# One piece of a down product moved behind the second group spot, sums of x one piece earlier, and the last unit's add of two copies moved up

## The chip, the cores and the metric

The kernel runs on one core of a Trainium2 chip, as a single launch. Its time is the device time of that core in microseconds (us). The engines of the core are named as the profile names them: TensorE (PE, with PEld for its weight loads), VectorE (DVE), ScalarE (ACT), GpSimd (POOL) and SyncE (SP). GpSimd issues the loads, SyncE issues the stores and the transposes done by DMA.

## The reference

Two layers follow each other. The first is attention with projected keys and values, over 8 batches, 8 heads, a sequence of 1024 and a head size of 64; keys and values are projected from 1024 rows to 64. The second is a maxout layer on the 8192 x 512 matrix that the attention gives.

```python
k_proj = einsum('ks,bhsd->bhkd', E, k)          # 64 x 64 for each head
v_proj = einsum('ks,bhsd->bhkd', F, v)
scores = matmul(q, k_proj.T) / sqrt(64)
attn   = exp(scores - max) / sum(exp(scores - max))
x      = matmul(attn, v_proj)                   # laid out as 8192 x 512
out    = maximum(x @ w1, x @ w2) @ w_out        # 512 -> 1024 -> 512, float32
```

The inputs are float32; the kernel computes in float16 with float32 accumulation.

## The kernel before

**The algebra.** `maximum(h1, h2)` is `relu(h1 - h2) + h2`. So the kernel works with `wd = w1 - w2` for the way up, and with `m = w2 @ w_out` for the part of the way down that needs no maximum: `out = relu(x @ wd) @ w_out + x @ m`. The way up and the way down are each done as a product of 2 x 2 blocks with seven products in place of eight (the Winograd form of Strassen's scheme). The names `p1` to `p7` in the code are these seven products; `s_x`, `s_g`, `t_w` and `T_sb` are the sums and differences of blocks of x, of the relu's output g, and of the weights that the scheme needs. The sums of x (`sums_x`) and of g (`sums_g`) are made by VectorE (line 519).

**Units.** A batch has two units, so there are sixteen, with the numbers 0 to 15; unit 1 is the second of batch 0 and unit 2 the first of batch 1. Each unit has an up phase (`up_steps`, matmuls at line 558) and a down phase (`down_steps`, matmuls at line 636). The down phase of unit n runs interleaved with the up phase of unit n + 1 and with attention for later units. Every down product is twelve matmuls, cut into three pieces of four (two pieces in unit 0, one in the last unit); so a unit has 21 down pieces, which are keyed `("P", n, product, piece)`, both counted from 0. The up phase has two halves of seven products each, keyed `("U", n, half, k)`. The order of the seven in both phases is 1, 2, 6, 5, 7, 3, 4.

**Group spots.** In each unit there are two places, `("G", n, 0)` and `("G", n, 1)`, at which attention work for one group of four heads stands: the scores of a new group (line 266) into the PSUM banks 2 and 3, and the sums and values of the group before it (line 278) into a pair of banks called `att`. ScalarE takes the exponential of the two score banks (line 355), then the logarithm of the sums (line 374); VectorE later multiplies the values by the inverse (line 381). At the second spot of unit 1 the sums and values stand ahead of the scores, and the scores there are the first of tile 2, whose `qt` comes from two DMA transposes that SyncE issues at the first spot of unit 1 (line 249).

**Banks.** The up products use banks 2 and 3, the same that the scores use; the first up product of the first half begins in bank 2, that of the second half in bank 3. The down products use banks 0 and 1. A product that is accumulated further must first be copied out of its bank: `keep` (line 529), on ScalarE. The first up product behind a group spot therefore waits until the exponential has emptied its bank, and the third up product of a half waits until the copy of the first is done.

**Order.** The order on every engine is written out by hand: a list `slots` is built once, each entry a piece, an up product or a spot, and `at_slot` hangs further work behind an entry (the sums, the projections of the next batch's k and v at line 180, their transposes at line 211, the loads). Engines keep this order and wait by semaphore. The list for unit n is made in the loop at lines 782 to 799: `x` pieces, the group spot, `y` pieces, then seven up products with one piece between each two. Unit 1 has its own pair of `(x, y)`.

**The last unit.** It has no up phase beside it. Product 7 (`p7`) is copied out as `u2`, product 5 as `s5`; product 3 (`p3`) is added to `u1` for the output block (0, 1), and then `u2 + s5` gives block (1, 1), both at line 660; product 4 is done in two halves, each added to `u2` (line 699). Every block is stored from SyncE as soon as it is added (line 651), blocks of 256 KB and the two halves of 128 KB.

Of the kernel before, what the change touches and what calls it, by code (L numbers as in the profile page):

```python
# [16 lines left out]
def kernel(  # L17
# [42 lines left out]
    def mm_bank(dtype=FP32, n=None):  # L60
        if n is None:
            n = turn.pop(0)
            turn.append(n)
        return ps.tile([128, 512 if dtype == FP32 else 1024], dtype, tag=f"mm{n}", name="mm_ps")
# [391 lines left out]
    U = {(b, o): {"n": n, "b": b, "o": o, "t": tiles[b]} for n, (b, o) in enumerate(units)}  # L456
# [28 lines left out]
    def s_g(i):  # L485
        return box[2].rearrange("q (s n m) -> q s n m", s=4, n=NG)[:, i]

    def s_x(i, u):
        n = u["n"] % 3
        half = box[1 if n < 2 else 3].rearrange("q (h s n m) -> q h s n m", h=2, s=4, n=NX)  # L490
        return half[:, n % 2, i]
# [10 lines left out]
    def x_blk(u, j, h):  # L502
        return u["t"]["xt"][:, h * NX : (h + 1) * NX, j, u["o"] * W : (u["o"] + 1) * W]

    def g_blk(u, j, h):
        if u["b"] == 0:
            return u["t"]["gt", u["o"]][:, h * NG : (h + 1) * NG, j * W : (j + 1) * W]
        return u["gt"][:, h * NG : (h + 1) * NG, j * W : (j + 1) * W]
# [18 lines left out]
    def keep(tag, bank, copy=nc.scalar.copy):  # L527
        x = ppool.tile([128, 512], FP32, tag=tag, bufs={"pu": 3, "pd": 4}[tag], name="p_sb")
        copy(out=x, in_=bank)  # L529
        return x  # L530
# [79 lines left out]
    def down_steps(u, alone):  # L610
        b, o = u["b"], u["o"]
        st = {}
        xbank, ybank = (0, 1) if u["n"] % 2 == 0 else (1, 0)

        def cat(g, x):
            return lambda n: g[:, n] if n < NG else x[:, n - NG]

        def product(k, name, n, lo=0, hi=2 * (NG + NX)):
            if n is not None and (lo == 0 or alone):
                st[name] = mm_bank(n=n)  # L620
            bank = st[name]
            A = lambda j, h: cat(g_blk(u, j, h), x_blk(u, j, h))
            S = lambda i: cat(s_g(i), s_x(i, u))
            Bb = lambda h, c: cat(
                wo_sb[:, h * NG : (h + 1) * NG, c * CH : (c + 1) * CH],
                m_sb[:, h * NX : (h + 1) * NX, c * CH : (c + 1) * CH],
            )
            T = lambda i: lambda n: T_sb[:, i, n, :]
            a, w_ = {
                1: lambda: (A(0, 0), Bb(0, 0)), 2: lambda: (A(0, 1), Bb(1, 0)),  # L630
                3: lambda: (S(3), Bb(1, 1)), 4: lambda: (A(1, 1), T(3)),
                5: lambda: (S(0), T(0)), 6: lambda: (S(1), T(1)), 7: lambda: (S(2), T(2)),
            }[k]()
            for m in range(lo, hi):
                i, c = divmod(m, NG + NX)
                nc.tensor.matmul(  # L636
                    out=bank[:, i * CH : (i + 1) * CH],
                    lhsT=a(c)[:, i * 128 : (i + 1) * 128],
                    rhs=w_(c),
                    start=(n is not None and m == (lo if alone else 0)),  # L640
                    stop=(c == NG + NX - 1), skip_group_check=True,
                )
            return bank

        two = lambda ap: ap.rearrange("q (i m) -> q i m", i=2)

        def o_tile():
            return opool.tile([128, 2, CH], FP32, tag="o", name="o_sb")

        def store(j, c, o_sb, i0=0, i1=2):  # L650
            nc.sync.dma_start(
                out=out.rearrange("(n p i o) m -> n o p i m", p=128, i=NI, o=2)[
                    b, j, :, 2 * o + i0 : 2 * o + i1, c * CH : (c + 1) * CH
                ],
                in_=o_sb[:, i0:i1],
            )

        def add(j, c, x, y):
            o_sb = o_tile()
            nc.vector.tensor_tensor(out=o_sb, in0=two(x), in1=two(y), op=ALU.add)  # L660
            store(j, c, o_sb)

        def keep_d(bank):
            return keep("pd", bank, *([nc.vector.tensor_copy] if u["n"] == 0 else []))

        size = 2 * (NG + NX) // (1 if alone else 2 if u["n"] == 0 else 3)

        def piece(k, name, n, m):
            product(k, name, n, m, m + size)

        def whole(k, name, n):
            return product(k, name, n, 2 * (NG + NX) - size)

        def p1():
            st["s1"] = keep_d(whole(1, "X", xbank))

        def p2():
            add(0, 0, whole(2, "Y", ybank), st["s1"])

        def p6():  # L680
            st["u1"] = keep_d(whole(6, "X", None))

        def p5():
            st["s5"] = keep_d(whole(5, "Z", ybank))

        def p7():
            st["u2"] = keep_d(whole(7, "X", None))

        def p3():
            add(0, 1, whole(3, "Z", None), st["u1"])  # L690
            add(1, 1, st["u2"], st["s5"])

        def p4():
            o_sb = o_tile()
            if alone:
                for i in range(2):
                    bank = product(4, ("C", i), 2 + i, 6 * i, 6 * i + 6)
                    part = slice(i * CH, (i + 1) * CH)
                    nc.vector.tensor_tensor(
                        out=o_sb[:, i], in0=bank[:, part], in1=st["u2"][:, part], op=ALU.add,  # L700
                    )
                    store(1, 0, o_sb, i, i + 1)
                return
            nc.scalar.copy(out=o_sb, in_=two(whole(4, "X", None)))
            store(1, 0, o_sb)

        steps_ = (
            (p1, 1, "X", xbank), (p2, 2, "Y", ybank), (p6, 6, "X", None), (p5, 5, "Z", ybank),
            (p7, 7, "X", None), (p3, 3, "Z", None), (p4, 4, "X", None),
        )  # L710
        return [
            (*(lambda a=a, m=m: piece(*a, m) for m in range(0, 2 * (NG + NX) - size, size)), f)
            for f, *a in steps_
        ]
# [67 lines left out]
    for n, key in enumerate(units):  # L782
        downs = down_steps(U[key], n == last)
        if n in (0, last):
            for p, pieces in enumerate(downs):
                slots += [(("P", n, p, i), x) for i, x in enumerate(pieces)]
            continue
        pieces = [(("P", n, p, i), x) for p, x in enumerate(downs) for i, x in enumerate(x)]
        ups = [*up_steps(U[units[n + 1]])]
        for h, (x, y) in enumerate(((3, 3), (2, 1)) if n == 1 else ((2, 2), (2, 3))):  # L790
            slots += pieces[:x]
            slots.append((("G", n, h), lambda: None))
            slots += pieces[x : x + y]
            del pieces[: x + y]
            for i in range(7):
                slots.append((("U", n, h, i), ups.pop(0)))
                if i < 6:
                    slots.append(pieces.pop(0))
        assert not pieces and not ups
# [3 lines left out]
    def at_slot(key, s, *a):  # L803
        steps.setdefault(key, []).append(lambda: s(*a))
# [47 lines left out]
    for b in range(3, B):  # L852
        t = tiles[b]
        n = 2 * b - 3
# [8 lines left out]
    for i, (new, old) in enumerate(zip([*groups[1:], none], groups)):  # L863
        n, h = divmod(i + 2, 2)
# [6 lines left out]
    for n, (b, o) in enumerate(units):  # L871
        u = U[b, o]

        if b == 0:
            where = ()
        elif n == 2:
            where = (("P", 1, 0, 2), 0), (("P", 1, 1, 0), 1), (("P", 1, 1, 2), 2), (("U", 1, 0, 1), 3)
        else:
            where = tuple((("U", n - 2, 1, k), i) for k, i in ((6, 2), (3, 0), (4, 1), (5, 3)))
        for key, i in where:  # L880
            at_slot(key, sums_x, u, (i,))

        if n:
            end = ("U", n - 1, 1, 6) if n > 1 else ("P", 0, 6, 1)
            m = 0 if n == last else 2
            for key, i in (end, 0), (("P", n, 0, 0), 1), (("P", n, 1, m), 2), (("P", n, 2, m), 3):
                at_slot(key, sums_g, u, (i,))
# [41 lines left out]
```

## Time and profile before

| | |
|---|---|
| median of 4 runs | 329.36 us (327.85 to 330.14) |
| the profiled execution's own time | 328.24 us |
| its span in the profile | 326.5 us |
| granted TensorE clock | 0.998 |
| TensorE busy | 317.0 us, 97% of the span |
| VectorE, ScalarE, GpSimd busy | 239.6, 201.1, 37.0 us |
| unit 1's down phase on TensorE | from about 64.5 to 84 us |
| last matmul begins; last engine work (VectorE) ends | 321.8; 322.8 us |

The span is what the hardware profiler shows of one execution; the execution's own time has some 1.7 us more around it. A line of the timeline gives start, duration, engine, line of the code, operation, what is written and read, and in brackets the idle time of that engine just before it and what ended that. A busy TensorE isn't the same as TensorE at its peak, since matmuls overlap and their ends are modelled; the steps from one start to the next are the better measure. PE and PEld are one engine's matmuls and its weight loads; `SPq` rows are DMA issues from SyncE.

### The profile page before, as it was taken

How to read it: one execution, taken by the hardware profiler on the slowest of the kernel's cores; microseconds unless marked ns; L12 is line 12 of the kernel's file. 1: busy time of each engine (PE TensorE's matmuls, PEld its weight loads, DVE VectorE, ACT ScalarE, POOL GpSimd, SP SyncE). 2: the span in 40 equal slices, each digit the busy share in tenths (PEclk: the TensorE clock that was granted, in tenths of full speed). 3: DMA queues.
4: the chain of work that ended last, by engine and by line, in shares of the span. 5: the costliest groups of instructions: out<-in, count | busy, mean ns of one | idle time of the engine just before them, and what ended most of it. 6: DMA issues, size and time to landing. Idle time of an engine off the chain costs nothing.

```text
span 326.5 us, 9015 instructions
## 1 busy us (share of the span) xinstructions
PE 317.0 (97%) x3856; PEld 248.6 (76%) x3856; DVE 239.6 (73%) x424; ACT 201.1 (62%) x359; POOL 37.0 (11%) x56
## 2 busy tenths in 40 slices
PE   7979999999999999999999999999999999999994
PEld 3544446877887788878887888878887888888883
DVE  1346898985969778677967796977967796969572
ACT  2365322666777577667776777657776777765541
POOL 8546002003000110003000300003000000000000
PEclk9999999999999999999999999999999999999999
DMA  8999999988999699997999599888999130312032
GB/s 147 204 197 191 206 207 208 218 197 150 194 238 233 115 158 238 202 187 97 215 217 180 110 187 243 190 163 125 228 192 214 37 99 32 98 34 98 33 131 96
DMA packets 74680, 53.14 MB, mean 163 GB/s; under 512 B 29456, under 2 KB 74512, under 8 KB 74640
## 3 DMA queue, kind: packets, MB, share of 16 engines
q0 software_dynamic: 29376, 28.31, 54.7%
q1 hardware_dynamic: 45264, 24.25, 30.7%
q8 instruction: 30, 0.49, 0.6%
q14 instruction: 10, 0.08, 0.1%
HBM read 57.15 MB, written 16.78 MB: 226 GB/s over the span
## 4 chain that ended last, share of the span: by engine, by line
PE 79%; DMA 13%; POOL 2%; DVE 2%; issue 1%; ACT 0%; DVEq 0%; POOLq 0%
PE mm_ps L636 44%; PE mm_ps L558 26%; DMA q_sb<-in_q_dram 8%; DMA v_sb<-in_v_dram 4%; PE att_ps L180 3%; PE att_ps L278 3%; PE mm_ps L266 3%; DMA big<-in_moe_w_dram 2%; POOL q_sb L102 1%; POOL k_sb L102 1%; DVE gt_sb L573 1%; PE mm_ps L237 1%; DVE o_sb L660 1%; POOL v_sb L102 1%; DVE xt_sb L381 0%
## 5 line engine op out<-in xcount | busy, mean ns | idle before, releaser
L529 ACT COPY p_sb<-mm_ps 128x512 f32<-128x512 f32 x172 | 97.1, 594 | 43.0 <-PE mm_ps L558 30.7
L636 PEld LDWEIGHTS <-big 128*128 128x128 f16 x768 | 73.5, 98 | 12.1 <-issue 3.5
L636 PE MATMUL mm_ps<-T_sb,big 128*128 128x256 f16 x576 | 77.9, 273 | 0.0
L573 DVE TENSOR_TENSOR gt_sb<-mm_ps,p_sb 128x512 f16<-128x512 f32 x56 | 38.5, 688 | 45.7 <-PE mm_ps L558 42.5
L558 PE MATMUL mm_ps<-big,big 128*128 128x256 f16 x336 | 50.4, 272 | 0.0
L558 PEld LDWEIGHTS <-big 128*128 128x128 f16 x448 | 43.8, 98 | 5.3 <-issue 0.2
L636 PEld LDWEIGHTS <-gt_sb 128*128 128x128 f16 x384 | 35.7, 98 | 9.6 <-issue 5.4
L636 PE MATMUL mm_ps<-wo_sb,gt_sb 128*128 128x256 f16 x256 | 42.9, 273 | 0.1
L558 PEld LDWEIGHTS <-wd_sb 128*128 128x128 f16 x336 | 32.9, 98 | 4.1 <-issue 0.4
L558 PE MATMUL mm_ps<-xt_sb,wd_sb 128*128 128x256 f16 x224 | 33.6, 273 | 0.2 <-ACT ex_sb L355 0.2
L355 ACT ACTIVATE ex_sb<-mm_ps 128x512 f16<-128x512 f32 x50 | 27.2, 597 | 9.6 <-PE att_ps L278 7.0
L381 DVE TENSOR_TENSOR xt_sb<-att_ps,ld_sb 128x1024 f16<-128x1024 f32 x26 | 31.7, 1219 | 0.1
L660 DVE TENSOR_TENSOR o_sb<-mm_ps,p_sb 128x512 f32<-128x512 f32 x32 | 21.9, 684 | 11.0 <-PE mm_ps L636 7.6
L636 PE MATMUL mm_ps<-m_sb,xt_sb 128*128 128x256 f16 x128 | 24.4, 273 | 0.0
L608 ACT ACTIVATE gt_sb<-mm_ps 128x512 f16<-128x512 f32 x28 | 16.8, 600 | 8.7 <-PE mm_ps L558 8.7
L519 DVE TENSOR_TENSOR big<-gt_sb 128x1024 f16<-128x1024 f16 x32 | 21.9, 685 | 0.2
L576 DVE TENSOR_SCALAR gt_sb<-gt_sb 128x512 f16<-128x512 f16 (+1 forms) x56 | 20.5, 366 | 1.9
L636 PE MATMUL mm_ps<-T_sb,gt_sb 128*128 128x256 f16 x128 | 21.5, 273 | 0.0
L636 PE MATMUL mm_ps<-wo_sb,big 128*128 128x256 f16 x128 | 21.5, 273 | 0.0
L636 PEld LDWEIGHTS <-xt_sb 128*128 128x128 f16 x192 | 18.8, 98 | 2.2
L229 POOL COPY junk<-kpt_sb 1x1 f16<-1x1 f16 x5 | 0.9, 176 | 162.0 <-DMA kpt_sb<-kp_sb 162.0
L573 DVE TENSOR_TENSOR gt_sb<-p_sb 128x512 f16<-128x512 f32 x28 | 19.1, 681 | 0.0
(85 smaller groups left out, 427.8 us busy)
## 6 DMA issues: line engine op xcount, KB each, us to landing
out_dram<-o_sb SPq DMA_DIRECT2D x63, 256.0 KB, 2.7
k_sb<-in_k_dram POOLq DMA_DIRECT2D x7, 1024.0 KB, 10.1
v_sb<-in_v_dram POOLq DMA_DIRECT2D x7, 1024.0 KB, 17.7
q_sb<-in_q_dram POOLq DMA_DIRECT2D x7, 1024.0 KB, 22.3
k_sb<-in_k_dram POOLq DMA_DIRECT2D x4, 256.0 KB, 6.8
q_sb<-in_q_dram POOLq DMA_DIRECT2D x4, 256.0 KB, 7.9
v_sb<-in_v_dram POOLq DMA_DIRECT2D x2, 512.0 KB, 12.5
big<-in_moe_w_dram POOLq DMA_DIRECT2D x8, 128.0 KB, 10.6
```

Of the source, the lines that this page charges most:

```text
L102: nc.gpsimd.dma_start(out=t[n][:, h0:h1], in_=src[b, h0:h1].rearrange("h (p c) d -> p h c d", c=NC),)
L180: nc.tensor.matmul(out=kv_ps[r * KP : (r + 1) * KP, 0:n], lhsT=eft[:, i, c, :], rhs=t[w][:, h0:h1, c, :], start=(c == 0), stop=(c == NC - 1),)
L355: nc.scalar.activation(out=t["ex", g, j][:, e, :], in_=banks[e], func=ACTF.Exp, scale=scale)
L381: nc.vector.tensor_tensor(out=x_out(t, g, j).rearrange("q z o n -> q o z n"), in0=at_ps.rearrange("q o (z n) -> q o z n", z=2), in1=ld[:, ...
L519: nc.vector.tensor_tensor(out=S(i), in0=x, in1=y, op=op)
L529: copy(out=x, in_=bank)
L558: nc.tensor.matmul(out=bank[:, m * W : (m + 1) * W], lhsT=w_[:, n_, (2 * d + m) * 128 : (2 * d + m + 1) * 128], rhs=a[:, n_, :], start=(n ...
L573: nc.vector.tensor_tensor(out=c_blk(j, c), in0=two(x), in1=two(y), op=ALU.add)
L576: nc.vector.tensor_scalar_max(ap, ap, 0.0)
L608: nc.scalar.activation(out=out, in_=in_, func=ACTF.Relu)
L636: nc.tensor.matmul(out=bank[:, i * CH : (i + 1) * CH], lhsT=a(c)[:, i * 128 : (i + 1) * 128], rhs=w_(c), start=(n is not None and m == (lo ...
L660: nc.vector.tensor_tensor(out=o_sb, in0=two(x), in1=two(y), op=ALU.add)
```

## The change

There are three edits.

1. In unit 1 the pairs `(x, y)` go from `(3, 3)` and `(2, 1)` to `(3, 2)` and `(2, 2)`. So unit 1 has two pieces instead of three between its first group spot and the up products, and two instead of one between its second spot and the up products. All pieces from the sixth on shift by one place against the up products; the second group spot comes one piece earlier, the first up product behind it stands where it stood.
2. The four sums of x for unit 2 are hung on entries by key. Three keys change by one piece each. In VectorE's order only sum 2 changes place by it: it comes ahead of the output add that ends the piece `("P", 1, 1, 2)`, which itself is the piece that moves behind unit 2's first up product.
3. In the last unit (`alone`) the add of the two copies `u2` and `s5`, with its store, moves from the end of `p3` to the end of `p7`, right behind the copy of `u2`.

No instruction is added or removed on any engine. GpSimd's and SyncE's instructions keep their order, but for the place of one store among the last five, that of block (1, 1), which comes ahead of that of block (0, 1).

```diff
         def p7():
             st["u2"] = keep_d(whole(7, "X", None))
+            if alone:
+                add(1, 1, st["u2"], st["s5"])
 
         def p3():
             add(0, 1, whole(3, "Z", None), st["u1"])
-            add(1, 1, st["u2"], st["s5"])
+            if not alone:
+                add(1, 1, st["u2"], st["s5"])
...
-        for h, (x, y) in enumerate(((3, 3), (2, 1)) if n == 1 else ((2, 2), (2, 3))):
+        for h, (x, y) in enumerate(((3, 2), (2, 2)) if n == 1 else ((2, 2), (2, 3))):
             slots += pieces[:x]
             slots.append((("G", n, h), lambda: None))
             slots += pieces[x : x + y]
...
         elif n == 2:
-            where = (("P", 1, 0, 2), 0), (("P", 1, 1, 0), 1), (("P", 1, 1, 2), 2), (("U", 1, 0, 1), 3)
+            where = (("P", 1, 0, 1), 0), (("P", 1, 0, 2), 1), (("P", 1, 1, 1), 2), (("U", 1, 0, 1), 3)
```

## The prediction

> **What bounds the kernel now.** I read the page from the top: the engines' shares, the 40 slices, the chain. TensorE is the engine to watch.
>
> ```profile
> PE 317.0 (97%) x3856; PEld 248.6 (76%) x3856; DVE 239.6 (73%) x424; ACT 201.1 (62%) x359; POOL 37.0 (11%) x56
> ...
> PE   7979999999999999999999999999999999999994
> ...
> PE 79%; DMA 13%; POOL 2%; DVE 2%; issue 1%; ACT 0%; DVEq 0%; POOLq 0%
> ```
>
> From the second tenth on TensorE has work in every slice (granted clock 0.998). The chain is TensorE's own for 79%; its DMA share lies before 54 us, where the edits don't reach. So the change can win only what TensorE still waits for behind 54 us, and what comes after its last matmul. I therefore read the timeline around the two edits. First, the second group spot of unit 1:
>
> ```profile
> 77.41 0.40 PE L266 MATMUL mm_ps<-qt_sb,kpt_sb 64*32 64x256 f16 x16
> ...
> 77.89 1.08 ACT L355 ACTIVATE ex_sb<-mm_ps 128x512 f16<-128x512 f32 x2 [0.93 <-PE mm_ps L266]
> ...
> 78.53 0.60 PE L558 MATMUL mm_ps<-xt_sb,wd_sb 128*128 128x256 f16 x4 [0.18 <-ACT ex_sb L355]
> ...
> 78.86 0.60 ACT L374 ACTIVATE ld_sb<-att_ps 128x512 f32<-128x512 f32 x1
> ...
> 79.33 1.10 ACT L529 COPY p_sb<-mm_ps 128x512 f32<-128x512 f32 x2
> ...
> 80.48 0.31 PEld L558 LDWEIGHTS <-big 128*128 128x128 f16 x3 [0.22 <-issue]
> ```
>
> The scores go to banks 2 and 3. One down piece later TensorE wants bank 3 for unit 2's next up product: its first weights stand loaded at 78.08, but the matmul starts at 78.53, when ScalarE's exponential has emptied the bank. Two up products further (80.17 wanted, 80.48 got) it waits again: the copy of that product (the second of the two at 79.33) stands in ScalarE's queue behind both exponentials, the logarithm and a down copy. Behind this the timeline shows TensorE only its 0.2 us changes of tile shape, up to the last unit. Then the end:
>
> ```profile
> 319.49 0.58 ACT L529 COPY p_sb<-mm_ps 128x512 f32<-128x512 f32 x1 [0.72 <-PE mm_ps L636]
> ...
> 320.86 0.69 DVE L660 TENSOR_TENSOR o_sb<-mm_ps,p_sb 128x512 f32<-128x512 f32 x1 [3.47 <-ACT p_sb L529]
> ...
> 321.46 0.68 DVE L660 TENSOR_TENSOR o_sb<-p_sb 128x512 f32<-128x512 f32 x1
> ...
> 321.69 0.38 PE L636 MATMUL mm_ps<-T_sb,xt_sb 128*128 128x256 f16 x2
> 322.06 0.75 DVE L699 TENSOR_TENSOR o_sb<-mm_ps,p_sb 128x256 f32<-128x256 f32 x2
> ```
>
> TensorE ends at 322.07. VectorE's four last adds run nearly back to back to 322.81. The stretch views and SyncE's rows show what follows:
>
> ```profile
> 316.22 0.37 SPq L651 DMA_DIRECT2D out_dram<-o_sb  x1
> ...
> 321.57 0.37 SPq L651 DMA_DIRECT2D out_dram<-o_sb  x1
> ...
> 322.17 0.37 SPq L651 DMA_DIRECT2D out_dram<-o_sb  x1
> ...
> 323.18 0.41 SPq L651 DMA_DIRECT2D out_dram<-o_sb  x1
> ```
>
> ```profile
> 322.00:322.50 0.50, 0.07 (x1) 0.00 (x0) 0.50 (x3) 0.00 (x0) 0.00 (x0) 1.00 0.04 14
> 322.50:323.00 0.50, 0.00 (x0) 0.00 (x0) 0.31 (x1) 0.00 (x0) 0.00 (x0) 1.00 1.01 326
> 323.00:323.50 0.50, 0.00 (x0) 0.00 (x0) 0.00 (x0) 0.00 (x0) 0.00 (x0) 1.00 1.05 350
> ```
>
> (The columns of the last three: stretch, length, busy PE, PEld, DVE, ACT, POOL, clock, DMA share, GB/s.) The four last stores leave SyncE at 321.57, 322.17, 322.64 and 323.18 and land 2.2, 2.3, 2.4 and 2.1 us later, the last at 325.28; the span ends at 326.5, 1.2 us on. Data flows from about 322.45 at 326 to 354 GB/s with no pause: 786 KB in 2.25 us, to 324.7, then some 0.5 us to the landing. So the tail is a queue of stores, not the last add alone.
>
> **Part 1, the moved piece.** No instruction is added or removed. Twelve matmuls of a down product go in three pieces of four; a piece takes 0.436 us (the timeline's steps: 78.97, 79.40, 79.84). One piece goes from before to behind the second group spot, so:
>
> The second spot starts 0.44 us earlier (scores 76.97 for 77.41, exponential 77.45 for 77.89), and bank 3 is free at 78.53 - 0.44 = 78.09. Its up product stands where it stood, since the piece now fills the place: 78.19. The wait of 0.34 is gone. The ScalarE queue keeps its order, so the copy that held the next wait ends 0.44 earlier, and that product starts at 80.04 for 80.48. TensorE's own pace would have it at 78.19 + 4 x 0.436 = 79.93, so about 0.1 us of wait stays. Sum: **0.44 us**, the piece itself, not the 0.65 of both waits. Ends: 0.1 (if a wait appears elsewhere) and 0.55 (if ScalarE's queue closes up wholly).
>
> What has to hold for this, each with its cover:
> - Behind the first spot unit 2's first up product starts after two pieces, 67.56 for 68.00. Its bank 2 is free when the first of the exponentials at 66.58 ends, about 67.17: 0.4 us spare. Unit 2's down phase has two pieces there also and shows no wait (weights at 86.82).
> - The projection of tile 2 (L180) moves from 69.40 to 68.96. Its v was issued at 51.05 and landed 13.4 us later, 64.5. The second spot needs the first transposed half of q: issued 71.10, landed 4.5 later at 75.6, wanted at 76.97. Spare 1.3 us. The POOL gate behind the second half (77.99) does not move, so the loads of tile 3 start as before.
> - VectorE: the sum of x with index 2 (0.42, of which 0.34 holds the queue) goes ahead of unit 1's output add, which waits for the moved piece: 68.76 for 68.32. That add's store is not late: SyncE is held by the q transposes from 71.10 and sends it at 75.50. Behind it on VectorE the sum of g goes from 68.92 to 69.36 (first wanted by product 7 near 77), unit 2's first add from 69.86 to 69.96 (its bank is wanted at 72.0), the last sum of x ends about 71.3. The cast of v's projection, which opens the chain cast, normalise, kpt copy, wants VectorE at 71.56 (72.00 less 0.44). It has 0.26 us spare; without it, each tenth lost is a tenth of TensorE at the kpt transposes.
> - ScalarE: the s5 copy of the moved row now stands behind the ReLU: about 76.45 to 77.03, ahead of the exponential at 77.45. Spare 0.4.
>
> No stall remains behind 81 us to swallow the gain: loads of tile 3 are wanted 24 us later. It arrives whole at 319 us.
>
> **Part 2, the last unit.** Times here without the shift of part 1. The add (1,1) needs only the copies; u2's ends at 320.07. VectorE has been idle since 317.4, takes it at 320.13 and is free at 320.73 (an add holds it 0.60). Product 3 ends at 320.76, so add (0,1) starts at 320.86 as now: nothing queued behind is late. First half of product 4: 321.46, when VectorE is free and the bank done (321.42). Second half: TensorE ends 322.07, add at 322.17 for 322.39. Stores leave SyncE at 320.84, 321.57, 322.03, and the last 0.15 behind its add's end at 322.59: 322.74 for 323.18, **0.44 us** sooner, as SyncE no longer has four issues of 0.37 to 0.45 on end.
>
> Then the landing. The lone store of 256 KB at 316.22 landed in 2.1 us; half the bytes at 350 GB/s are 0.37 less: 1.72. With (1,1) gone at 322.47, (0,1) flows to 323.2, the first half to 323.57, and the last finds free engines: 322.74 + 1.72 = 324.47 for 325.28, a gain of **0.81**. The Trainium skill (DMA: Bandwidth & Descriptors, "Anatomy of one DMA — SWDGE (gpsimd) path") speaks against that: it gives a DMA a constant 2.0 us plus its bytes at 436 GB/s, whatever is queued. By it the last store takes 2.3 us in both kernels and only the 0.44 of issue is won. It is fitted on the other issue path, and here 256 KB took 2.1 in all, less than the rule's 2.6; I take the row. Ends: 0.44 and 0.85.
>
> Sum: 0.44 + 0.81 = 1.25 us, 326.5 to 325.25 of span and 328.24 to 327.0 of that execution, with the 1.74 around it. The median of the runs shown is 1.12 higher than that execution; the same saving gives 329.36 - 1.25 = **328.1 us**, 0.4% faster.
>
> **Rivals.** *Only the tail (or its issue) pays*: TensorE's wait reappears, say on the q half if q of tile 2 lands 1.3 us later. For it: all loads up to 71 us come through busy DMA. Against it: the spare above. Gain 0.44 to 0.81, 328.5 to 328.9. *Nothing*: both gains hidden, the last landing set by a fixed latency and a late issue; 329.4. Against it: the stores' data plainly queue. *Slower*: VectorE's queue in unit 1. If the output add now waits long for its moved piece, the cast, the normalise, the kpt copy behind it are late, and with them the kpt transposes. From 0.26 us of delay TensorE pays; from 0.26 + 1.25 = 1.5 us the kernel is slower, and two further add times of 0.69 on top, 2.9 in all, would make 330.8. No row shows such a delay.
>
> **Chances.** A difference of 0.5%, 1.65 us, is about what a measurement of this kernel can tell from none; the four runs alone spread over 2.3 us. My case 0.76, its own range 327.3 to 328.7: 0.37 of it beyond 1.65 us by scatter and the upper ends, 0.39 within. Only the tail 0.11 (0.02 faster, 0.09 within). Nothing 0.06 (0.01, 0.04, and 0.01 slower). Slower 0.07 (0.06 and 0.01 within). Faster 0.40, same 0.53, slower 0.07. The range takes in my case with scatter, the tail alone and no change: 326.9 to 329.6.
>
> **What would show it.** Right: no idle weight load at the first up product behind unit 1's second spot, one of at most 0.15 us two products on; the piece's 0.44 still ahead at 100 and 300 us; VectorE adding the two copies while product 3 runs; the last store leaving 0.65 to 0.7 us behind the end of TensorE's last matmul (now 1.1) and landing in 1.7. Wrong: a new wait at the kpt transposes or the scores of the second spot, or a last store still taking 2.1 us.

## The result, and the profile after

The changed kernel takes 328.16 us (median of 44 runs, 326.44 to 330.2) against 329.07 us (63 runs, 327.37 to 331.5) for the kernel before on the same chip. The ratio is 0.997, with a 95% interval of 0.9959 to 0.9981: some 0.9 to 1.0 us less. 328.1 was predicted. That the two agree to 0.1 us is in part luck: the sum took 1.25 us off a median of 329.36 over four runs, and with more runs the kernel before stands 0.29 lower and the saving is 0.91. Behind it, one term of the sum was a little too large, and three waits that the prediction had not seen came to light.

The profiled execution of the changed kernel has a span of 326.4 us, against 326.5 before, and TensorE is busy for 97% of it, as before. From this alone one would say that nothing was won. So a comparison of spans is too coarse here, and the stretches have to be compared one by one. I measure each from a fixed mark. The mark for all that follows unit 1 is its first group spot's first score matmul, which starts at 66.00 us before and at 65.78 after (the 0.22 between them comes from the loads at the start, which differ from one execution to the next). The mark for the tail is the modelled end of TensorE's last matmul, at 322.07 before and 322.73 after.

**Unit 1's second spot.** The timeline of the changed kernel, to be set beside that of before in the prediction:

```profile
77.23 1.08 ACT L355 ACTIVATE ex_sb<-mm_ps 128x512 f16<-128x512 f32 x2 [0.50 <-PE mm_ps L266]
...
77.97 0.60 PE L558 MATMUL mm_ps<-xt_sb,wd_sb 128*128 128x256 f16 x4
...
79.61 0.53 PEld L558 LDWEIGHTS <-big 128*128 128x128 f16 x4
...
79.83 0.60 PE L558 MATMUL mm_ps<-big,big 128*128 128x256 f16 x4
```

From the mark, the exponential starts at 77.23 - 65.78 = 11.45 (before 11.89), the first up product behind it at 12.19 (before 12.53, with a wait that is now gone), and the third one at 14.05 (before 14.48). The four weight loads at 79.61 take 0.53 us where such a group takes 0.42 elsewhere; this is the 0.1 us of wait that is left.

**The tail.** The timeline of the changed kernel's last microseconds:

```profile
320.77 0.69 DVE L660 TENSOR_TENSOR o_sb<-p_sb 128x512 f32<-128x512 f32 x1 [2.72 <-ACT p_sb L529]
...
321.46 0.69 DVE L660 TENSOR_TENSOR o_sb<-mm_ps,p_sb 128x512 f32<-128x512 f32 x1
...
322.11 0.42 DVE L702 TENSOR_TENSOR o_sb<-mm_ps,p_sb 128x256 f32<-128x256 f32 x1
...
322.35 0.38 PE L636 MATMUL mm_ps<-T_sb,xt_sb 128*128 128x256 f16 x2
322.77 0.42 DVE L702 TENSOR_TENSOR o_sb<-mm_ps,p_sb 128x256 f32<-128x256 f32 x1 [0.23 <-PE mm_ps L636]
```

The add of the two copies now runs while TensorE works on product 3, and VectorE waits 0.23 us for the last matmul where before it was behind. SyncE's rows and the view by stretches (the columns are those of the prediction):

```profile
321.49 0.37 SPq L651 DMA_DIRECT2D out_dram<-o_sb  x1
...
322.18 0.91 SPq L651 DMA_DIRECT2D out_dram<-o_sb  x2
...
323.22 0.36 SPq L651 DMA_DIRECT2D out_dram<-o_sb  x1
```

```profile
322.50:323.00 0.50, 0.23 (x3) 0.00 (x0) 0.27 (x2) 0.00 (x0) 0.00 (x0) 1.00 1.01 330
323.00:323.50 0.50, 0.00 (x0) 0.00 (x0) 0.19 (x1) 0.00 (x0) 0.00 (x0) 1.00 1.05 350
323.50:324.00 0.50, 0.00 (x0) 0.00 (x0) 0.00 (x0) 0.00 (x0) 0.00 (x0) 1.00 1.03 352
```

The row of two at 322.18 holds the stores of block (0, 1) and of the first half of product 4. From the end of the last matmul, stores leave and land so (us; a landing is the last of the store's sixteen completions):

| | four stores leave | last landing | end of the span |
|---|---|---|---|
| before | -0.50, 0.10, 0.56, 1.11 | 3.23 | 4.39 |
| after | -1.25, -0.56, -0.09, 0.49 | 2.48 | 3.63 |

The tail is 0.75 us shorter, and it is the same in every profile of a kernel with this edit (3.63 to 3.66).

**Where the 1.19 went.** 0.44 + 0.75 = 1.19 us should have shown in the span. 0.10 of the 0.44 is lost at once. Unit 2's first spot, the next after the edited place, starts 19.04 behind the mark (before 19.38), which is 0.34 earlier and not 0.44. VectorE's ReLU behind the second spot is the row that differs. Before:

```profile
80.23 0.91 POOL L102 DMA_DIRECT2D q_sb<-in_q_dram  x1
...
81.19 0.29 DVE L576 TENSOR_SCALAR gt_sb<-gt_sb 128x512 f16<-128x512 f16 x1
```

and after:

```profile
80.01 0.91 POOL L102 DMA_DIRECT2D q_sb<-in_q_dram  x1
...
80.53 0.51 DVE L576 TENSOR_SCALAR gt_sb<-gt_sb 128x512 f16<-128x512 f16 x1
```

Against the mark, GpSimd's third load issue for tile 3 stands where it stood (14.23), and the ReLU comes 0.44 earlier, so that it now starts while that issue runs. It takes 0.51 us for 0.29. All that follows on VectorE is some 0.2 late by it, down to the add (line 573) that empties a bank for the scores of unit 2's first spot. Ten of the profiles, this one among them, have unit 1's edit. In six of them the ReLU is lengthened, by 0.03 to 0.35 us, and it ends 0.11 to 0.12 behind the end of the load issue in all six. VectorE has some 0.12 to spare here: lengthenings of 0.03, 0.16, 0.16, 0.21, 0.22 and 0.35 put unit 2's first spot 0, 0.04, 0.04, 0.09, 0.10 and 0.23 later. In the other four, and in the four kernels without the edit, the ReLU takes 0.29. So this is a price of the edit, paid in those executions in which the load issue, which starts 13.27 to 14.59 behind the mark, falls at the wrong moment. No run moves that issue alone, so the cause is read from these ends, and why the two engines should hold each other up isn't shown.

The remaining 0.34 is kept up to 143 us behind the mark. Then, at the second spot of the unit where batch 6's keys are first used, the weight loads of the changed kernel say:

```profile
219.37 0.21 PEld L278 LDWEIGHTS <-vp_sb 64*32 64x32 f16 x16
221.10 0.14 PEld L266 LDWEIGHTS <-kpt_sb 64*32 64x32 f16 x16 [1.52 <-DMA kpt_sb<-kp_sb]
```

and those of the kernel before, in its profile:

```profile
220.13 0.10 PEld L266 LDWEIGHTS <-kpt_sb 64*32 64x32 f16 x3
220.46 0.13 PEld L266 LDWEIGHTS <-kpt_sb 64*32 64x32 f16 x13 [0.23 <-issue]
```

TensorE waited 1.5 us for a DMA transpose that in the other profile had landed in time. This costs some 1.2 us at TensorE's end. From the mark to the last matmul's end it is therefore 256.95 us after, against 256.08 before, although it was 0.44 ahead at unit 1's second spot. The experiments had to tell whether the change brings this wait.

### The profile page after: what moved, and what is told of

Read it like the earlier page. It is cut to its first block, busy times and chain, and to the rows that moved or that the text cites. A ratio compares the mean times of both kernels' runs of the same rounds, so it can differ in the third digit from the quotient of the medians.

```text
span 326.4 us, 9015 instructions
## 1 busy us (share of the span) xinstructions
PE 317.4 (97%) x3856; PEld 248.6 (76%) x3856; DVE 239.9 (74%) x424; ACT 200.9 (62%) x359; POOL 37.0 (11%) x56
## 4 chain that ended last, share of the span: by engine, by line
PE 79%; DMA 13%; POOL 4%; DVE 2%; issue 1%; SPq 0%; POOLq 0%; DVEq 0%
PE mm_ps L636 44%; PE mm_ps L558 25%; DMA q_sb<-in_q_dram 8%; DMA v_sb<-in_v_dram 4%; PE att_ps L180 3%; PE att_ps L278 3%; PE mm_ps L266 3%; DMA kpt_sb<-kp_sb 1%; POOL big L126 1%; POOL k_sb L102 1%; POOL q_sb L102 1%; DVE gt_sb L573 1%; PE mm_ps L237 1%; DVE o_sb L660 1%; POOL v_sb L102 0%
```

## The experiments

### Unit 1's edit alone

```diff
 (the changed kernel, without its third edit)
             st["u2"] = keep_d(whole(7, "X", None))
-            if alone:
-                add(1, 1, st["u2"], st["s5"])
 
         def p3():
             add(0, 1, whole(3, "Z", None), st["u1"])
-            if not alone:
-                add(1, 1, st["u2"], st["s5"])
+            add(1, 1, st["u2"], st["s5"])
```

> Unit 1's edits alone (the moved piece and the three keys of the sums of x), the last unit as before. My theory: the second group spot comes 0.44 us earlier, the first up product behind it finds its bank free (no idle weight load; 0.35 us before), the third one waits 0.1 us or less (0.22 before), and the 0.44 us are kept to the end: ratio to before 0.9987, and TensorE's last matmul 0.44 us earlier when measured from the scores at the first spot of unit 1. The tail behind the last matmul stays as it was, 4.4 us from the last matmul's end to the end of the span. Rival (only the tail pays): a new wait behind the second spot eats it, ratio 1.000, and the distance from the first spot to the last matmul is unchanged.

Measured: 328.71 us (14 runs), ratio 0.9997, interval 0.9977 to 1.0016. From the mark, the exponential at 11.45, unit 2's first spot at 18.94 (before 19.38), the end of TensorE at 255.64 (before 256.08); tail 4.40. Batch 6's transpose was in time in this profile, and the 0.44 of the prediction arrives whole, 240 us later (the ReLU is lengthened by 0.03 only). The time alone can't show a gain of 0.13%; it doesn't contradict it either.

### The last unit's edit alone

```diff
 (the changed kernel, with before's unit 1)
-        for h, (x, y) in enumerate(((3, 2), (2, 2)) if n == 1 else ((2, 2), (2, 3))):
+        for h, (x, y) in enumerate(((3, 3), (2, 1)) if n == 1 else ((2, 2), (2, 3))):
...
-            where = (("P", 1, 0, 1), 0), (("P", 1, 0, 2), 1), (("P", 1, 1, 1), 2), (("U", 1, 0, 1), 3)
+            where = (("P", 1, 0, 2), 0), (("P", 1, 1, 0), 1), (("P", 1, 1, 2), 2), (("U", 1, 0, 1), 3)
```

> The last unit's edit alone (the add of two copies and its store at the end of product 7), unit 1 as before. My theory: the last store leaves SyncE 0.67 us behind the end of the last matmul (1.1 before) and lands 1.7 us later (2.1 before); the span ends 0.8 us closer to the last matmul, 3.6 us for 4.4; ratio 0.9975. Rival (each store takes a fixed time from its issue, whatever is queued): the last store still takes 2.1 us, the gain is 0.44 us, ratio 0.9987. Rival (nothing): ratio 1.000 and the last landing as far behind the last matmul as before.

Measured: 328.46 us (22 runs), ratio 0.9978, interval 0.9961 to 0.9995. Tail 3.65 for 4.39; the last store leaves 0.49 behind the last matmul and takes 2.01 us, for 0.67 and 1.7 expected. Exponential at 11.89 as before. TensorE waited for batch 6's transpose here too, and from the mark to its end it is 256.98: the wait came without the edit in unit 1.

### Both edits, but the early block's store left where it was

```diff
         def p7():
             st["u2"] = keep_d(whole(7, "X", None))
             if alone:
-                add(1, 1, st["u2"], st["s5"])
+                st["o11"] = o_tile()
+                nc.vector.tensor_tensor(
+                    out=st["o11"], in0=two(st["u2"]), in1=two(st["s5"]), op=ALU.add
+                )
...
+            if alone:
+                store(1, 1, st["o11"])
+            else:
```

> The changed kernel, but the early add of the two copies is stored where it was stored before, behind the store of block (0,1). It tells whether the tail's gain comes from VectorE's free queue or from the 256 KB that flow early. My theory (the queue of stores sets the end): stores leave at about 321.6, 322.0, 322.5, 322.95 in the times of before, 786 KB flow from 0.9 us behind the first one at 350 GB/s, and the last landing is only 0.05 to 0.1 us earlier than before: the tail from the last matmul is 4.3 us, and the whole ratio is that of unit 1's edit, 0.9985. Rival (fixed time from issue): the last issue is 0.23 us earlier than before, so is the end. Rival (VectorE's last add sets the end): 0.22 us of tail gain. Both give 4.15 to 4.2 us behind the last matmul, ratio 0.998.

Measured: 328.58 us (22 runs), ratio 1.0001, interval 0.9985 to 1.0018 (0.9985 expected; this profile has the late transpose and 0.09 of the ReLU's delay). VectorE's adds are as early as in the changed kernel:

```profile
320.19 0.69 DVE L690 TENSOR_TENSOR o_sb<-p_sb 128x512 f32<-128x512 f32 x1 [2.72 <-ACT p_sb L529]
...
322.19 0.42 DVE L707 TENSOR_TENSOR o_sb<-mm_ps,p_sb 128x256 f32<-128x256 f32 x1 [0.23 <-PE mm_ps L636]
```

Yet the stores leave at -0.55, -0.13, 0.43, 0.97 from the last matmul's end, the last lands at 3.19, and the tail is 4.35. An early add without its early store is worth 0.04 us. So of the 0.75, nearly all lies in the store.

### The early block's store on ScalarE's queue, the add where it was

```diff
 (the kernel before, with)
-        def store(j, c, o_sb, i0=0, i1=2):
-            nc.sync.dma_start(
+        def store(j, c, o_sb, i0=0, i1=2, q=nc.sync):
+            q.dma_start(
...
-            store(j, c, o_sb)
+            if alone and (j, c) == (1, 1):
+                store(j, c, o_sb, q=nc.scalar)
+            else:
+                store(j, c, o_sb)
```

> The kernel before, with the store of the last unit's block (1,1) issued from ScalarE's queue in place of SyncE's; nothing else moved. It splits the tail into issue and data. SyncE then has three issues instead of four: the last one leaves at the end of VectorE's last add plus 0.15, 0.9 us behind the last matmul's end (1.1 before). My theory (the 786 KB in the queue set the end): the last landing stays at 3.2 us behind the last matmul's end, within 0.1. Rival (a fixed time from the issue): it comes 0.2 us earlier, at 3.0. For the late completion at 217 us: if the edit of the last unit brings it about, this kernel, which has no such edit, does not show it.

Measured (one run): 327.61 us. Stores leave at -0.50, 0.11, 0.44 and 0.87, so the last leaves 0.24 earlier than before, since SyncE has one issue less to make. It lands at 3.24, as before (3.23): it now takes 2.37 us for 2.12. The tail stays 4.40. With the first of the four stores where it was, an earlier issue of the last gives nothing: the bytes in front of it set when it lands.

Four kernels side by side, first store and last landing: -0.50 and 3.23 (before), -0.50 and 3.24 (this one), -0.55 and 3.19 (early add, late store), -1.25 and 2.48 (after). In all four, the last landing is 3.73 to 3.74 behind the first issue. The tail is a queue of fixed length that starts when the first block's store leaves. This holds while the queue doesn't run dry: in the changed kernel the second store leaves 0.69 behind the first, whose 256 KB take some 0.75 us at 350 GB/s, so by this estimate a first store that left much earlier still would gain little.

### The changed kernel and the kernel before again

No edit; the changed kernel twice, timed, and the kernel before once, for its profile.

> The changed kernel again, for a second profile and in the same rounds as its parts. In its first profile TensorE waited 1.5 us for one kpt transpose that landed 4.5 us behind its issue, where the others took 2.7 to 2.9. If that is chance, this profile has no such wait (or has it in another place), the distance from the first spot of unit 1 to the last matmul is 0.44 us shorter than in the kernel before, and the ratio is 0.996 to 0.997, the product of the two parts. If the change brings it about, the same transpose of the same batch is late again.

> The kernel before once more, for its profile. In four profiles of kernels with the last unit's edit, one of the sixteen completions of one kpt transpose (the fourth of five, issued at about 217 us) came 1.5 to 1.8 us behind the other fifteen, while a fetch of TensorE's instructions ran, and TensorE waited 1.2 to 1.5 us at the second spot; in the two profiles without that edit (before, and unit 1 alone) it did not. If that is chance from one execution to the next, this profile may show it too (in about two of three, by the six so far); if the edit brings it about, all completions come 2.5 to 2.9 us behind the issue.

> The changed kernel a third time, beside the one above. The traces give its gain without late completions as 0.44 us in unit 1 and 0.75 us behind the last matmul, 1.2 us, ratio 0.9964; timed so far 0.997 and 0.998. If the late completion at 217 us strikes the kernel before as often (it did in one of its two profiles), it takes nothing from the mean, and this ratio lies between 0.996 and 0.998. If it strikes the changed kernel more often (five of five profiles of kernels with both edits unaltered would then show it), the ratio stays at 0.997 or above and this profile has it.

Measured: the changed kernel 328.12 us (22 runs; ratio 0.9982, interval 0.9967 to 0.9997) and 327.71 us (22 runs; 0.9969, interval 0.9953 to 0.9984), the kernel before 328.5 in its one run. The wait for batch 6's transpose stood in all three profiles. The weight load in that of the kernel before:

```profile
220.70 0.14 PEld L266 LDWEIGHTS <-kpt_sb 64*32 64x32 f16 x16 [1.20 <-DMA kpt_sb<-kp_sb]
```

So the wait comes without the change too. The view of DMA work around this transpose shows what differs. Columns of the first row: packets, MB, share of 16 engines' time in a stretch of 3.3 us before and 4.7 us after; the last figure of the second row is the us from issue to landing. In the first profile of the kernel before:

```profile
q8 instruction: 1, 0.02, 2.3%
...
kpt_sb<-kp_sb SPq DMA_TRANSPOSE x1, 2.7
```

and in that of the changed kernel:

```profile
q8 instruction: 1, 0.02, 1.2%
...
kpt_sb<-kp_sb SPq DMA_TRANSPOSE x1, 4.5
```

The transpose reports by sixteen completions. In both, fifteen of them have come 2.7 us after the issue; the sixteenth comes at 2.73 in the one and at 4.52 in the other. This happened at the same transpose only, that of batch 6, in 7 of the 11 profiles that have it in this place: with the kernel before in one of two, with unit 1's edit in five of seven, without it in two of four. By the last unit's early add it is six of seven, without it one of four, and all three profiles of the changed kernel have it; eleven profiles are too few to tell whether it strikes both kernels equally often. One more thing is near it in time, always: a fetch of 16 KB of instructions (the queue named "instruction"; the expectations call it TensorE's, but no view says whose it is), which starts 2.1 to 2.5 us behind the issue and takes about 1 us. When the sixteenth completion was late, that fetch had started at 2.08 to 2.15 (2.52 in one); when in time, at 2.28 to 2.30. That the fetch holds up the part of the transpose that finishes last is argued from this coincidence; no view shows on which DMA engine either lay.

### Old places for the sums of x, and one piece more

```diff
 (the changed kernel, with the kernel before's keys)
-            where = (("P", 1, 0, 1), 0), (("P", 1, 0, 2), 1), (("P", 1, 1, 1), 2), (("U", 1, 0, 1), 3)
+            where = (("P", 1, 0, 2), 0), (("P", 1, 1, 0), 1), (("P", 1, 1, 2), 2), (("U", 1, 0, 1), 3)
```

> The changed kernel with the three keys of the sums of x as they were, so that the piece moves alone. My theory: the keys are worth nothing; the sum with index 2 stands behind the output add again, the last sum of x still ends before the cast wants VectorE, no idle weight load appears behind the second spot of unit 1, and the distance from the scores at the first spot to the exponential at the second is that of the changed kernel, 11.45 us. Rival (the sums are what lets the piece move): TensorE waits at the third up product behind the first spot or at the kpt transposes, and the distance is longer by 0.1 us or more. The late completion at 217 us appears if the last unit's edit is its cause.

```diff
 (the changed kernel, with two pieces behind the second spot moved, not one)
-        for h, (x, y) in enumerate(((3, 2), (2, 2)) if n == 1 else ((2, 2), (2, 3))):
+        for h, (x, y) in enumerate(((3, 1), (2, 3)) if n == 1 else ((2, 2), (2, 3))):
```

> The changed kernel with one piece more moved: one piece left behind the first spot of unit 1, three behind the second. My theory (the gain is the covered wait, not the piece): the second spot comes up to 0.44 us earlier again, but there is no wait left behind it, so that nothing more than 0.1 us is won up to the fourth up product of the second half; and the first up product behind the first spot now comes at the moment when its bank is freed, so 0 to 0.1 us is lost there. Sum 0.0, from -0.1 to +0.2 us, between the scores at the first spot and the start of unit 2's scores. Rival (each piece moved is worth 0.44 us): that distance is 0.44 us shorter than in the changed kernel.

Measured (one run each): 326.45 us with the old keys; unit 2's first spot at 18.94 and TensorE's end at 255.64, as with the new ones in the run with unit 1's edit alone. The sums of x leave no mark: edit 2 is worth nothing, to 0.01 us. With a second piece moved, 328.65 us (with the late completion); the exponential starts another 0.33 earlier, at 11.12, and unit 2's first spot stands at 18.95. The wait that a piece can fill was gone with the first; the second changes places, and nothing else.

### The projection of batch 6 one product earlier

```diff
-        at_slot(("U", n, 0, 1), step_kv, t, 0, H, "kv", True, True)
+        at_slot(("U", n, 0, 0 if b == 6 else 1), step_kv, t, 0, H, "kv", True, True)
```

> The changed kernel with one more edit: for batch 6 alone, whose kpt transpose had the late completion, the projection of k and v stands one up product earlier, so that the transpose is issued about 0.9 us sooner; nothing is added. In six of ten profiles so far TensorE waited 1.2 to 1.5 us there, and without the late completion the transpose landed only 0.3 us before TensorE wanted it. My theory: with the late completion TensorE now waits 0.3 to 0.6 us at most, without it not at all; 0.9 us is won in six of ten executions, 0.5 us on average, against the changed kernel in the same rounds, and the ratio to before is 0.9955 to 0.996. Rival (the fetch goes along: the late completion follows TensorE's instruction count, not the transpose's issue): the transpose is then over before the fetch, no completion is late, with the same gain. Rival (it costs elsewhere, VectorE's order changes by it): the distance from unit 1's first spot to the last matmul is longer than 255.64 us though no completion is late.

Measured: 328.24 us (22 runs), ratio 0.9968, interval 0.9952 to 0.9983: not better than the changed kernel beside it (0.9969), where 0.5 us was expected. The transpose did land well before it was wanted, by 2.2 us, and TensorE waited for none. But its timeline shows, in the same unit:

```profile
216.62 0.69 DVE L573 TENSOR_TENSOR gt_sb<-mm_ps,p_sb 128x512 f16<-128x512 f32 x1
...
217.37 0.60 PE L558 MATMUL mm_ps<-big,big 128*128 128x256 f16 x4 [0.49 <-DVE gt_sb L573]
```

The casts and copies of the projection now stand on VectorE ahead of the add that empties an up product's bank, and TensorE waits 0.49 us for that add. This takes the place of the wait that was removed: 256.18 from the mark (counted from the same score matmul) to TensorE's end. So a place further ahead only trades one wait for another, and VectorE's order is tried next.

### k before v

```diff
             def finish_v():
-                nc.vector.tensor_copy(out=t["vp"][KP:128, h0:h1], in_=zd(kv_ps[KP:128, 0:n]))
                 if dma:
                     nc.vector.tensor_copy(out=kp[:, :, 1, :], in_=kp[:, :, 0, :])
                     step_kpt_dma(t)
+                nc.vector.tensor_copy(out=t["vp"][KP:128, h0:h1], in_=zd(kv_ps[KP:128, 0:n]))
```

> The changed kernel, with VectorE's doubling of the projected k (0.29 us) and the transpose of kpt ahead of the cast of v (0.69 us), in batches 3 to 7. Theory (the transpose lands 0.3 us before it is wanted, and its last completion is 1.5 to 1.8 us late in more than half of the profiles): it leaves about 0.7 us sooner, so it is wanted 1.0 us behind its usual landing. If the last completion of batch 6 is late again, TensorE waits 0.5 to 0.8 us at the second spot in place of 1.2 to 1.5; if not, not at all. From unit 1's first scores to TensorE's end 255.64, or 256.2 with a late completion. In time about 0.4 us off the changed kernel, ratio to before 0.9955 if its own is 0.9970. Rival 1 (the lateness follows the transpose, as the fetch of instructions and it share something that moves along): wait 1.2 again, 256.9. Rival 2 (a new wait takes its place, as in the run with the projection early): 256.1 with no late completion.

Then the same two lines still further ahead, outside the deferred function, so that they come before VectorE's output add:

```diff
+            if dma:
+                nc.vector.tensor_copy(out=kp[:, :, 1, :], in_=kp[:, :, 0, :])
+                step_kpt_dma(t)
+
             def finish_v():
                 nc.vector.tensor_copy(out=t["vp"][KP:128, h0:h1], in_=zd(kv_ps[KP:128, 0:n]))
-                if dma:
-                    nc.vector.tensor_copy(out=kp[:, :, 1, :], in_=kp[:, :, 0, :])
-                    step_kpt_dma(t)
```

> As the run with k first, but the doubling of k and the transpose stand also ahead of the output add that VectorE makes in this place (0.69 us), at the price that VectorE waits here for ScalarE's cast of k (about 0.1 us) and that the add's store follows the transpose. Theory: the transpose of batch 6 leaves 1.4 us sooner, so it is wanted 1.7 us behind its usual landing; a late last completion (1.5 to 1.8) costs TensorE at most 0.1 us; 255.64 to 255.75 from unit 1's first scores to its end in either case. In time 0.5 to 0.8 us off the changed kernel: ratio to before 0.995 if its own is 0.997. Rival 1 (the add that comes 0.4 later holds a bank that TensorE wants): a wait of up to 0.4 in each of five batches, 256 to 257.6. Rival 2 (the transpose so early meets those of q and is itself slower): completions later than 2.7 us behind the issue in every batch.

Measured: k first 326.41 us (6 runs), ratio 0.9935, interval 0.9914 to 0.9956, below both kernels (the changed one had 0.9959 to 0.9981 and, on this chip, 0.9967 to 0.9997), though with few runs and not beside the changed one; k ahead of the add too 327.67 us (15 runs), ratio 0.9955, interval 0.9940 to 0.9969. In neither profile does TensorE wait for the transpose. In batch 6 it lands 1.17 us (k first) and 1.47 us ahead of the scores, where it was some 0.4. Neither profile had a sixteenth completion that was late, so that the spare would have covered one is not shown.

With k first, TensorE's end stands at 255.07 from the mark, 0.57 less than with unit 1's edit alone (255.64), which none of the expectations had. It comes in five steps of 0.12 to 0.13, one at the second spot of each unit that takes a new batch's keys, less 0.04 that the ReLU loses at unit 2's first spot. The timeline of the kernel with unit 1's edit alone, at the first of them:

```profile
106.88 0.69 DVE L660 TENSOR_TENSOR o_sb<-mm_ps,p_sb 128x512 f32<-128x512 f32 x1 [1.30 <-PE mm_ps L636]
107.60 0.69 DVE L196 CAST vp_sb<-att_ps 64x512 f16<-64x512 f32 x1
...
111.39 0.68 DVE L573 TENSOR_TENSOR gt_sb<-mm_ps,p_sb 128x512 f16<-128x512 f32 x1
...
112.13 0.13 PEld L266 LDWEIGHTS <-kpt_sb 64*32 64x32 f16 x13 [0.23 <-issue]
```

and with k first:

```profile
106.99 0.69 DVE L660 TENSOR_TENSOR o_sb<-mm_ps,p_sb 128x512 f32<-128x512 f32 x1 [1.30 <-PE mm_ps L636]
107.60 0.28 DVE L197 COPY kp_sb<-kp_sb 64x512 f16<-64x512 f16 x1
...
111.38 0.68 DVE L573 TENSOR_TENSOR gt_sb<-mm_ps,p_sb 128x512 f16<-128x512 f32 x1
...
111.92 0.33 PEld L266 LDWEIGHTS <-kpt_sb 64*32 64x32 f16 x16
```

VectorE has no idle time from the output add to the add at line 573, the seventh instruction behind it. That last add reads one of the two banks that the scores go to, and the third score matmul waits for VectorE's semaphore; its record starts at 112.13, when the add that began at 111.39 has ended (112.07). So the 0.23 us that the profile calls "issue" is partly a wait for VectorE's queue. The cast of v starts 0.72 us behind the output add's start, that is after the add's 0.69 have ended; a copy of k in its place starts 0.61 behind it, before the add has ended, and the add at line 573 follows 4.39 behind it in place of 4.51: 0.12 earlier against TensorE. Why the cast waits for the add's end and the copy doesn't isn't shown. With the two lines ahead of the add, VectorE's order is another, and only 0.14 in all is won.

## Why the prediction was right

**Unit 1's piece: as worked out, 0.44 us.** The exponential was forecast 11.45 behind the first spot's scores, the first up product at 12.19, the third at 14.04 with some 0.1 of wait left; measured 11.45, 12.19 and 14.05. The piece, not the two waits of 0.65, was the right sum: it is what both profiles without a late completion show at TensorE's end (255.64 for 256.08). The covers named held: the sum of x that goes ahead of the output add cost nothing at the kpt transposes, as the run with the old keys shows. The rival in which only the tail pays falls with this, and so does the slower one: the cast that it would delay comes 0.43 earlier (5.57 behind the mark for 6.00).

What the covers left out is the ReLU behind the second spot. The prediction saw that GpSimd's loads of tile 3 stay where they are, and took this for safe; it didn't ask what on VectorE moves into them. Of the ten profiles with the edit, five keep 0.44 at unit 2's first spot within 0.01, and the others 0.40 to 0.21.

**The tail: mechanism right, 0.75 for 0.81.** VectorE takes the copies' add while product 3 runs, as forecast. The term that was off is the landing of the last store. It was to leave 0.67 behind the last matmul and land in 1.72 us, finding free engines. It left at 0.49, since VectorE starts its add 0.04 behind the matmul and SyncE follows 0.03 behind that add, for 0.10 and 0.15 in the sum; and it took 1.99, since the engines weren't free: the DMA share stays at 1.01 to 1.05 until 324. The two errors, 0.18 early and 0.27 long, nearly cancel, and not by chance: as the run on ScalarE's queue shows, a store that leaves earlier into a full queue only takes longer. The better account is that of the four kernels above: the first store leaves 0.75 earlier, and the landing follows 3.73 behind it.

**The rule weighed against the row.** The Trainium skill (DMA: Bandwidth & Descriptors, "Anatomy of one DMA — SWDGE (gpsimd) path") gives one DMA of that path a constant 2.0 us beside its bytes; that the constant holds however much is queued was the prediction's reading. By that estimate the gain is that of the last issue: 0.44 as forecast, 0.62 with the issue as measured (1.11 to 0.49). The measured gain is 0.75, and on ScalarE's queue an issue won 0.24 and the landing nothing. Where the stores stand in a queue of bytes, the row decides, and the constant doesn't.

**"No stall remains behind 81 us to swallow the gain": wrong.** The prediction looked for what the edits make late, and found nothing; it didn't ask how little slack the unchanged transposes have. The one of batch 6 usually lands some 0.4 us before the scores start, and when its sixteenth completion is 1.5 to 1.8 late, TensorE's end moves by 0.9 to 1.2. The kernel before has it as well, so it isn't a cost of the change alone; whether the change makes it more frequent stays open. It makes one profile of each kernel a poor measure: here it hid, with the ReLU's 0.10, the whole 1.19. There were also five waits of about 0.12 for VectorE in plain sight, under the name "issue", which the prediction read as changes of tile shape.

**Against the time.** 1.19 of 328.24, the kernel before's own profiled execution, is a ratio of 0.9964; measured 0.9970, 0.9982 and 0.9969, each with an interval that reaches about 0.15% to either side, so within them or just beside (the second ends at 0.9967). That the kernels can't be told apart more sharply has a second cause in the profiles: unit 1's first spot starts between 65.4 and 67.2 us, by the loads at the start, in kernels that are the same up to there. The parts alone gave 0.9997 and 0.9978; the first is at the limit of what can be measured, and its 0.44 rests on the traces.

## What to carry to other kernels

When a tail is a queue of stores, ask when the first of them leaves and how many bytes follow, not how late the last one is: an add moved up counts only through the store behind it. When a wait is filled by moving work behind it, the gain is at most the smaller of the wait and the work, and a second piece is worth nothing; then ask what else comes earlier with it, and what that runs into. Before a difference of spans is believed, walk both traces from a common mark and look for the first place where they part: here that was a ReLU beside a load issue, and then a transfer with 0.4 us to spare, in both kernels.

## What the runs showed of the hardware that was not expected

- A DMA transpose's completions are not of one piece: in 7 of 11 profiles, fifteen of the sixteen of batch 6's came at 2.7 us and the last at 4.2 to 4.5, beside a 16 KB instruction fetch of about 1 us. The other four transposes of the same kind in each of these profiles came whole at 2.6 to 2.8.
- A store of 128 KB took from 1.99 to 2.37 us from issue to landing in the same place, by how many bytes lay ahead of it. Its queue drained at 330 to 352 GB/s.
- On VectorE, behind an output add of 0.69 us, the cast of v out of PSUM started 0.72 us after the add's start and the copy of k between SBUF tiles 0.61 after it, in all five batches.
- VectorE's ReLU on 128x512 in SBUF took 0.32 to 0.64 us for 0.29 where it started while GpSimd issued a load, and ended 0.11 to 0.12 behind the end of that issue, in six profiles. Where it started only 0.17 behind the issue's start (k ahead of the add), it took 0.29, and the issue 0.94 for 0.91.
